# Masked attention and a rational FFN on one Trainium2 core: the rational function in monic form with three buffers per group, a constant scale in the mask, and a new order

## The chip, the cores and the metric

The kernel runs on one core of one Trainium2 chip. The metric is the device time in microseconds (us) of one execution; less is better. The engines of a core work side by side and are named as in the profile: PE is the matmul engine (PEld its weight load), DVE the vector engine, ACT the scalar engine, POOL the GpSimd engine, SP the sync engine, which here only issues DMAs.

## The reference

Two stages, on q, k, v of shape (8, 8, 576, 64): batch, heads, positions, head width. The arrays and the result are 32-bit floats.

```python
scores = scale * q @ k.T                        # per batch and head, 576 x 576, scale = 1/8
thresh = max(scores) - tau                      # per row, tau = 0.02
scores = where(scores >= thresh, scores, -1e9)
attn = exp(scores - max(scores))
attn = attn / (sum(attn) + 1e-9)
x = attn @ v                                    # 4608 tokens x 512

h = x @ w_in                                    # 512 x 2048
P = a0 + a1*h + a2*h**2 + a3*h**3
Q = 1 + |b0|*|h| + |b1|*h**2
g = P / (Q + 1e-6)
out = g @ w_out                                 # 2048 x 512
```

## The kernel before, in words

**Attention.** A unit is a pair of heads and a block of 128 query rows (`full`, both heads together), or the 64 rows that are left of 576 (both heads in one). `f_qk` (lines 734 to 757) makes the scores in three PSUM banks, `f_max` (763, 765) takes the negated row maximum, and `f_thr` (767 to 772) turns it into the number that the mask needs. `f_pre` (774 to 778) applies the mask with one Prelu of a huge slope: what lies over the threshold stays as it is, what lies below becomes hugely negative. `f_sum` (780 to 782) takes the exponential in place and sums each row on the way; its bias `ntau` shifts the kept scores back. `f_rec` and `f_rec2` make the reciprocal of the sum. Then the weights are split in two 16-bit parts, `hi` (`f_hi`, helper line 300 or 302) and `lo` (`f_lo`, 804), transposed by DMA on SP's queue (`f_tp`, 814), and multiplied by the split V (`f_av`, 873). The first batch, whose pairs are `plain`, does it with PE transposes and 32-bit matmuls instead (lines 817 to 857). `f_xh` and `f_xl` put the result into an x chunk: 256 token columns of all four head pairs.

**Weights.** w_in and w_out arrive as 64-bit words and are decoded on ACT and DVE in pieces of 128 rows (`decode_ops`, 422 to 474), sixteen of each; POOL issues their loads (490, 529). w_in is scaled and split into two 16-bit parts, every second row block of w_out into two parts of another format.

**FFN.** `moe_ops` (957 to 1154) works on a group: one x chunk and four blocks of 128 columns of w_in, so 128 x 1024 numbers of h. `f_g1` (988) makes h in PSUM, `f_h` (997) scales it into a buffer `t`. Then comes the rational function on 128 x 1024: `f_A` |h| (1002 on ACT or 1004 on DVE); `f_t1` b1 |h| + b0 (1009 or 1011); `f_r` a3 h + a2 (1016 or 1018); `f_r2` (helper line 307) and `f_r3` (1033) the rest of the numerator; `f_q` (1024) the rest of the denominator; `f_ln` and `f_inv` (1027, 1030) a first reciprocal as exp(-ln Q); `f_e`, `f_n` (1036, 1039) one Newton step on it; `f_g` (1042) the quotient, negated. `f_gh`, `f_gl` split half of it, and `f_g2` (1059, 1063) multiplies by w_out into two accumulators, one per 128 tokens, over all sixteen blocks of a chunk. `f_o` (1068, 1073) takes the sum out with a factor of -1, `f_st` stores it. A group takes four `t` buffers here (h, A, q, r), of ten, which it shares with the weight loads.

**The order.** It is worked out when the program is built. Every step is an `op` with an engine (or several with a duration on each, the table `FLEX`), a duration, a due time `key` in units of attention blocks, the steps it follows, and the buffers and PSUM banks it takes and gives back (`Hold`). `Plan.order` (148 to 243) runs a list schedule over these numbers: at each step the engine that can begin first takes, among what can begin about then (`TOL`), the step with the smallest key; a step with several engines goes to the one where `sooner` sees an earlier, priced end (`EARLY` until `EARLY_END`, then `PRICE`). Each engine then executes its steps in that order. Where PE would stand idle before `WARM_END`, dummy matmuls are put in (line 1205). `LEAD`, `SPACE0`, `SPACING`, `ENDK`, `ENDS`, `WHEN` and `AHEAD_RANK` set the due times of FFN groups and weights; `BA`, `BH` and `B1` list the PSUM banks that accumulators, h and other results may take; `plan.rank` sets who is served first with buffers.

Of the kernel before, what the change touches and what calls it, by code (L numbers as in the profile page):

```python
# [19 lines left out]
QC = 1.0 + 1e-6  # L20

POOLS = {"e": 3, "hi": 2, "pT": 2, "st": 8, "sc": 2, "t": 10, "u": 3, "g": 2, "x": 3, "xr": 1}
# [29 lines left out]
STEEP = 2.0 ** 100  # L54

PLAIN = (0, 1, 2, 3, 4)

UP = 2.0 ** -14
TPD = 1.3

AHEAD_RANK = 2.6933

# [8 lines left out]
        "ev": {"ACT": 0.465, "DVE": 0.6}, "ev1": {"ACT": 0.156, "DVE": 0.196}, "A": {"ACT": 0.583, "DVE": 0.341},  # L71
        "r": {"ACT": 0.666, "DVE": 0.4015}, "r2": {"DVE": 0.6075},
# [6 lines left out]
TOL = {"PE": 0.08, "ACT": 0.129, "DVE": 0.1, "POOL": 0.1, "DMA": 0.0, "GD": 0.0}  # L79
WARM, WARM_END = 0.6, 400.0  # L80
# [170 lines left out]
def masked_attention_rational_ffn(  # L251
# [16 lines left out]
    P = 128  # L268
# [37 lines left out]
    def tensor_tensor(dst, x, y, how):  # L306
        engines[plan.eng].tensor_tensor(dst, x, y, how)  # L307
# [10 lines left out]
    def place(h):  # L318
        return places[h.pool][h.slot]
# [9 lines left out]
    cv = cf[:, 8:16]  # L329
    qscale, taue = cv[:, 2:3], cv[:, 3:4]  # L330
    ident = const.tile([P, P], F32, name="ident")
# [3 lines left out]
    ones = bass.AP(one.tensor, one.offset, [list(one.ap[0]), [0, P]])  # L335
    qc = cv[:, 5:6]
    nc.vector.memset(qc, QC)

# [6 lines left out]
    for t in KKs:  # L345
        nc.gpsimd.memset(t[0:D, S:QW], 0.0)
        nc.gpsimd.memset(t[D:P, 0:REM], 0.0)
    nc.vector.tensor_scalar(qscale, cf[:, 6:7], 0.0, SCALE, ALU.is_ge, ALU.mult)
    nc.vector.tensor_scalar(cv[:, 4:5], cf[:, 6:7], 0.0, None, ALU.is_lt)
    nc.vector.scalar_tensor_tensor(taue, cf[:, 6:7], 0.0, cv[:, 4:5], ALU.max, ALU.add)  # L350

    nc.vector.tensor_scalar(taue, taue, 110.0, None, ALU.min)
    ntau = cv[:, 6:7]
    nc.vector.tensor_scalar(ntau, taue, -1.0, None, ALU.mult)
    a0, a1, a2, a3 = (cf[:, i:i + 1] for i in range(4))
    b0, b1 = cv[:, 0:1], cv[:, 1:2]

    def load_coefficients():
# [6 lines left out]

    def scale_ops(key, get, up, inv, s, after, tag):


        box = {}
        plan.rank = key  # L370
        h, hd, hb = Hold("sc", 1), Hold("u", 1), Hold("b", 1, B1)
# [104 lines left out]
    def w_key(i, j):  # L476
        k, step = WHEN[i]
        return k + j * step
# [3 lines left out]
    for i in range(NW):  # L482
# [18 lines left out]
        key = w_key(i, NC)  # L501
        sd = scale_ops(key, lambda i=i: wm[:, i * NC:(i + 1) * NC], 14, sw[:, i:i + 1], sw[:, NW + i:NW + i + 1], [x[3] for x in pieces], f"w{i}")
        sw_done.append(sd)
# [124 lines left out]
    def load_v_ops(bp):  # L628
# [35 lines left out]
        if pr == NP - 1:  # L664
            isx_done[bb] = scale_ops(p if bb else 4.0, lambda: vms[bb], 14, isx[:, bb:bb + 1], sx[:, bb:bb + 1], vm_ops[bb], f"x{bb}")
# [31 lines left out]
    xh_hold = {}  # L697
    x_done = {}

# [11 lines left out]
    def unit_ops(bp, t):  # L711
# [18 lines left out]
        def ev(hh):  # L730
            e = box["e"][:, hh * S:(hh + 1) * S]
            return e
# [34 lines left out]
        def f_thr(h0, h1):  # L767
            d, m = box["st"][:, 2 + h0:2 + h1], box["st"][:, h0:h1]
            if plan.eng == "ACT":
                nc.scalar.activation(d, m, AF.Identity, scale=qscale, bias=taue)  # L770
            else:
                nc.vector.tensor_scalar(d, m, qscale, taue, ALU.mult, ALU.add)  # L772

        def f_pre(hh):

            if hh == 0:
                box["e"] = place(e_hold)
            nc.scalar.activation(ev(hh), box["s"][hh], AF.Prelu, scale=qscale, bias=box["st"][:, 2 + hh:3 + hh], alpha=STEEP)  # L778
# [163 lines left out]
        if plain:  # L942
            av = op("PE", 2.36 if full else 0.76, p + 1.2, f_avp, two["tp"] + [v_loaded[bp]], [bh] + first, [two["pT"], vh_[bp]])
            plain_av.setdefault(bp, []).append(av)
        else:
            av = op("PE", 1.86 if full else 0.69, p + 1.2, f_av, two["tp"] + [v_low(bp)], [bh] + first, [two["pT"], vh_[bp]])
        xh = op(FLEX["xh" if full else "xhr"], 0, p + 1.4, f_xh, [av, isx_done["up"]] + ([x_done[ck][0]] if not first else []), (), [bh])
# [5 lines left out]
    accs = {}  # L953
    last_g1, last_g2 = [], {}
    sums = {}

    def moe_ops(ck, f0, nb, p, begins, ends, soon):
# [41 lines left out]
        def f_A():  # L999
            box["A"] = place(hA)[:, 0:FW]  # L1000
            if plan.eng == "ACT":
                nc.scalar.activation(box["A"], box["h"], AF.Abs)
            else:
                nc.vector.tensor_single_scalar(box["A"].bitcast(I32), box["h"].bitcast(I32), 0x7FFFFFFF, ALU.bitwise_and)

        def f_t1():
            box["q"] = place(hq)[:, 0:FW]
            if plan.eng == "ACT":
                nc.scalar.activation(box["q"], box["A"], AF.Identity, scale=b1, bias=b0)  # L1009
            else:  # L1010
                nc.vector.tensor_scalar(box["q"], box["A"], b1, b0, ALU.mult, ALU.add)

        def f_r():
            box["r"] = place(hr)[:, 0:FW]
            if plan.eng == "ACT":
                nc.scalar.activation(box["r"], box["h"], AF.Identity, scale=a3, bias=a2)  # L1016
            else:
                engines[plan.eng].tensor_scalar(box["r"], box["h"], a3, a2, ALU.mult, ALU.add)

        def f_r2():  # L1020
            tensor_tensor(box["r"], box["r"], box["h"], ALU.mult)

        def f_q():
            nc.vector.tensor_mul(box["q"], box["q"], box["A"])  # L1024

        def f_ln():
            nc.scalar.activation(box["A"], box["q"], AF.Ln, bias=qc)

        def f_inv():
            nc.scalar.activation(box["A"], box["A"], AF.Exp, scale=-1.0)  # L1030

# [3 lines left out]
        def f_e():  # L1035
            nc.vector.scalar_tensor_tensor(box["q"], box["q"], QC, box["A"], ALU.add, ALU.mult)  # L1036

        def f_n():
            nc.vector.scalar_tensor_tensor(box["q"], box["q"], -2.0, box["A"], ALU.add, ALU.mult)

# [24 lines left out]
        def f_o(tt, old):  # L1065
            if old:
                o = old[0]["o"]
                nc.vector.scalar_tensor_tensor(o, acc[tt], -1.0, o, ALU.mult, ALU.add)
            else:
                o = place(obox[tt]["hold"])  # L1070
                if not through:
                    o = o[:, tt * DM:(tt + 1) * DM]
                nc.scalar.activation(o, acc[tt], AF.Copy, scale=-1.0)  # L1073
            obox[tt]["o"] = o
# [173 lines left out]
```

## Time and profile before

| | |
|---|---|
| median of 3 runs | 1326.07 us (1324.98 to 1326.12) |
| span of the profiled execution | 1325.7 us |
| PE busy | 1291.3 us (97%), 9144 matmuls |
| PEld busy | 873.6 us (66%) |
| DVE busy | 1227.0 us (93%), 2043 instructions |
| ACT busy | 1178.6 us (89%), 2166 instructions |
| POOL busy | 244.2 us (18%), 468 instructions |
| mean granted PE clock | 0.992 |

A group of the profile is a line of the kernel on one engine: what it writes and reads, its shapes, how often it ran (x), its busy time in all, the mean duration of one in ns, and behind the second bar how long the engine was idle just ahead of it and what ended that. `cf` holds the per-partition constants (coefficients, tau), `st` the row statistics, `t` the buffers of the FFN, `banks` PSUM. A stretch (window) lists the busy time and the number of instructions of each engine within it, the clock that PE was granted (1.00 is full), the busy share of the DMA engines and GB/s. Busy PE time contains the dummy matmuls and matmuls at a lowered clock.

### The profile page before, as it was taken

What the parts mean: (1) busy time and instruction counts of PE and PEld (TensorE: products, weight loads), DVE (VectorE), ACT (ScalarE), POOL (GpSimd) and SP (SyncE); (2) the same over time, 40 slices, a digit from 0 to 9 for tenths busy, and PEclk for the clock granted to TensorE, in tenths of its full rate; (3) what the DMA queues carried; (4) which work ended last, traced back from release to release, by engine and by line L of the source; (5) the groups of instructions that cost most, each with busy time, mean ns of one, the idle gap of its engine ahead of it and who ended that gap; (6) DMA issues with size and microseconds to landing.
All of it is one profiled execution on the core that took longest, in us unless ns stands there. A gap on an engine that the chain in (4) does not pass through costs nothing. (4 is left out here: it accounts for less than half of the span.)

```text
span 1325.7 us, 24897 instructions
## 1 busy us (share of the span) xinstructions
PE 1291.3 (97%) x9144; PEld 873.6 (66%) x9144; DVE 1227.0 (93%) x2043; ACT 1178.6 (89%) x2166; POOL 244.2 (18%) x468
## 2 busy tenths in 40 slices
PE   8989899999999999999998999999999999999998
PEld 6657576666666666666666656666666766667775
DVE  6979899999999999999998899999999999987966
ACT  7979799999998999999998799999999999985764
POOL 2110000022212221332113231322213221100000
PEclk9989999999999999999999999999999999999999
DMA  8441544565656666666647465756657674550000
GB/s 266 136 139 50 167 90 78 123 152 112 134 102 116 131 109 119 125 140 116 115 100 136 78 133 101 143 101 142 110 119 130 110 139 104 103 102 1 16 17 16
DMA packets 340586, 146.63 MB, mean 111 GB/s; under 512 B 316208, under 2 KB 323184, under 8 KB 340464
## 3 DMA queue, kind: packets, MB, share of 16 engines
q1 hardware_dynamic: 316400, 86.49, 37.1%
q0 software_dynamic: 22784, 57.31, 15.5%
q8 instruction: 72, 1.18, 0.4%
q10 hardware_dynamic: 1280, 1.25, 0.4%
q14 instruction: 50, 0.41, 0.1%
HBM read 60.30 MB, written 9.44 MB: 53 GB/s over the span
## 5 line engine op out<-in xcount | busy, mean ns | idle before, releaser
L988 PEld LDWEIGHTS <-wi 128*128 128x128 f16 x3456 | 333.5, 98 | 71.8 <-issue 34.1
L988 PE MATMUL banks<-x,wi 128*128 128x256 f16 x3072 | 360.2, 273 | 2.7 <-ACT t L997 2.7
L1063 PE MATMUL banks<-wp,t 128*128 128x512 f32 x576 | 278.9, 600 | 3.4 <-DVE t L1042 3.3
L1059 PE MATMUL banks<-wp,g 128*128 128x512 f32 x864 | 275.8, 450 | 2.1 <-DVE g L1050 1.6
L778 ACT ACTIVATE e<-banks,st,cf 128x576 f32<-128x576 f32 x288 | 234.2, 827 | 14.6 <-DVE st L772 11.8
L782 ACT ACTIVATE e<-e,cf 128x576 f32<-128x576 f32 x288 | 221.3, 775 | 0.1
L804 DVE SCALAR_TENSOR_TENSOR e<-e,st,hi 128x576 f16<-128x576 f32 x252 | 204.5, 811 | 7.6 <-ACT hi L300 6.5
L1059 PEld LDWEIGHTS banks<-wp,g 128*128 128x128 f32 x864 | 158.2, 189 | 78.2 <-issue 38.6
L763 DVE TENSOR_REDUCE st<-banks 128x2 f32<-128x1152 f32 x128 | 172.2, 1346 | 9.4 <-PE banks L757 8.4
L300 ACT ACTIVATE hi<-e,st 128x576 f16<-128x576 f32 x199 | 151.6, 769 | 30.4 <-DVE st L793 20.9
L753 PE MATMUL banks<-KK,QQ 64*128 64x512 f32 x512 | 152.4, 641 | 2.1 <-ACT e L778 1.9
L1063 PEld LDWEIGHTS banks<-wp,t 128*128 128x128 f32 x576 | 101.2, 190 | 73.3 <-issue 59.2
L997 ACT ACTIVATE t<-banks,hsc 128x512 f32<-128x512 f32 (+1 forms) x192 | 106.2, 576 | 24.1 <-PE banks L988 23.8
L873 PEld LDWEIGHTS <-V 128*64 128x64 f16 x2520 | 103.1, 111 | 29.1 <-issue 27.6
L873 PE MATMUL banks<-pT,V 128*64 128x256 f16 (+1 forms) x2520 | 120.6, 249 | 0.5 <-DVE x L889 0.5
L757 PEld LDWEIGHTS banks<-KK,QQ 128*128 128x128 f32 x256 | 38.1, 188 | 97.0 <-issue 87.9
L598 POOL DMA_DIRECT2D QQ<-in_qT_dram x42 | 22.6, 538 | 424.9 <-PE banks L744 255.3
L1042 DVE SCALAR_TENSOR_TENSOR t<-t,cf,t 128x1024 f32<-128x1024 f32 (+1 forms) x73 | 92.4, 1266 | 0.8
L1033 DVE SCALAR_TENSOR_TENSOR t<-t,cf,t 128x1024 f32<-128x1024 f32 (+1 forms) x73 | 92.3, 1265 | 0.5
L1036 DVE SCALAR_TENSOR_TENSOR t<-t,t 128x1024 f32<-128x1024 f32 (+1 forms) x73 | 87.9, 1204 | 3.4 <-ACT t L1030 3.4
L307 DVE TENSOR_TENSOR t<-t,t 128x1024 f32<-128x1024 f32 (+1 forms) x73 | 87.9, 1204 | 1.6 <-ACT t L1016 1.2
L1024 DVE TENSOR_TENSOR t<-t,t 128x1024 f32<-128x1024 f32 (+1 forms) x73 | 87.9, 1204 | 1.0 <-ACT t L1009 0.8
(124 smaller groups left out, 1816.3 us busy)
## 6 DMA issues: line engine op xcount, KB each, us to landing
t<-in_w_in_dram POOLq DMA_DIRECT2D x16, 512.0 KB, 5.6
t<-in_w_out_dram POOLq DMA_DIRECT2D x16, 512.0 KB, 4.9
out_dram<-u POOLq DMA_DIRECT2D x26, 256.0 KB, 3.1
V<-in_v_dram POOLq DMA_DIRECT2D x24, 256.0 KB, 4.0
QQ<-in_qT_dram POOLq DMA_DIRECT2D x42, 144.0 KB, 2.8
KK<-in_kT_dram POOLq DMA_DIRECT2D x42, 144.0 KB, 3.0
QQ<-in_qT_dram POOLq DMA_DIRECT2D x42, 128.0 KB, 2.7
KK<-in_kT_dram POOLq DMA_DIRECT2D x42, 128.0 KB, 2.7
```

Of the source, the lines that this page charges most:

```text
L300: nc.scalar.activation(dst, src, AF.Identity, scale=factor)
L753: nc.tensor.matmul(d, QQ[r, t * P:(t + 1) * P], KK[r, REM:S], **one)
L763: nc.vector.tensor_reduce(box["st"][:, 0:2], box["both"], AX.X, ALU.max, negate=True)
L778: nc.scalar.activation(ev(hh), box["s"][hh], AF.Prelu, scale=qscale, bias=box["st"][:, 2 + hh:3 + hh], alpha=STEEP)
L782: nc.scalar.activation(e, e, AF.Exp, bias=ntau, accum_out=box["st"][:, 4 + hh:5 + hh])
L804: nc.vector.scalar_tensor_tensor(box["lo"][:, c], ev(hh), box["st"][:, 6 + hh:7 + hh], box["hi"][:, c], ALU.mult, ALU.subtract)
L873: nc.tensor.matmul(dst, V[:, c * P + hh * D:c * P + (hh + 1) * D], rhs, start=c == 0 and n == 0, stop=c == NT and n == 2)
L988: nc.tensor.matmul(d, wi_tile(c, f0 + j, hl), x[:, c, :], start=c == 0 and n == 0, stop=c == NC - 1 and n == 2)
L997: nc.scalar.activation(box["h3"][:, 2 * k:2 * k + 2, sl], psv[:, :, sl], AF.Identity, scale=hsc[:, b2, g:g + 1])
L1042: nc.vector.scalar_tensor_tensor(box["r"], box["r"], a0, box["q"], ALU.add, ALU.mult)
L1059: nc.tensor.matmul(acc[tt], fr(g[:, x]), fr(wo[f][y]), start=begins and j == n == 0, stop=ends and j == nb - 1 and n == 2)
L1063: nc.tensor.matmul(acc[tt], box["r"][:, o:o + P], wo[f], start=begins and j == 0, stop=ends and j == nb - 1)
```

## The change

The rational function is rewritten so that the leading coefficients are 1. A small step `monic`, once at the start, divides the coefficients: numerator a_i / a3, denominator b0 / b1 and (1 + 1e-6) / b1, with guards for tiny values, and puts -a3 / b1 into `osc`. Then h (h + a2) and |h| (|h| + bc) each come out of one DVE instruction, and `f_t1` and `f_r` are gone. `f_o` multiplies by `osc` in place of -1. The reciprocal is written over `h` (`box["i"] = box["h"]`), and |h| directly into the buffer of q: a group takes three `t` buffers. For that `f_ln` now follows `f_r3`. `f_e` reads its constant from `qc`, a per-partition operand.

In attention the scale of the mask and of the threshold is the constant 1/8 instead of the per-partition `qscale`; the exponential no longer has the bias `ntau`, and takes `passes` (1 or 0, by the sign of tau) as a per-partition scale.

The order: accumulators may take banks 3, 4 and 5, no longer 6; due-time constants, engine prices, one tolerance and the assumed duration of the mask are new; FFN groups have strictly rising ranks; the first attention result that goes into an x chunk now comes ahead of the others of that chunk; the scale steps of w_in are ranked earlier.

The core of the diff:

```diff
-B2, B3, BA, B1, BH = [(0, 1, 2), (3, 4, 5)], [(0, 1, 2)], [(3,), (4,), (5,), (6,)], [(7,), (6,), (5,)], [(5,), (6,)]
+B2, B3, BA, B1, BH = [(0, 1, 2), (3, 4, 5)], [(0, 1, 2)], [(3,), (4,), (5,)], [(7,), (6,), (5,)], [(5,), (6,)]
-LEAD, SPACE0, SPACING = 2.6322, 2.8866, 2.0262
-ENDK, ENDS = 5.3663, 11.0901
-WHEN = [(-3.6826, 2.0326), (5.7416, 0.8046), (12.6147, 0.2389), (15.0409, 0.8184)]
-V0, V1 = -1.5278, 1.1622
+LEAD, SPACE0, SPACING = 2.3618, 2.8866, 2.0262
+ENDK, ENDS = 6.3041, 10.3733
+WHEN = [(-4.5639, 2.0326), (5.966, 0.8046), (12.6147, 0.2389), (15.3809, 0.834)]
+V0, V1 = -1.2774, 1.1622
-AHEAD_RANK = 2.6933
+AHEAD_RANK = 2.4556
-EARLY = {"ACT": 1.5503, "DVE": 2.8692}
-EARLY_END = 792.5446
-PRICE = {"ACT": 0.7875, "DVE": 2.2723}
+EARLY = {"ACT": 1.7178, "DVE": 2.8692}
+EARLY_END = 1001.6266
+PRICE = {"ACT": 0.885, "DVE": 2.1934}
...
+    def monic():
+        t, u, a3 = (co_[:, i:i + 1] for i in range(6, 9))
+        nc.vector.tensor_scalar(t, b0, 2.0 ** -40, TINY, ALU.mult, ALU.max)
+        nc.vector.tensor_tensor(t, b1, t, ALU.max)
+        nc.vector.reciprocal(u, t)
+        nc.vector.tensor_tensor(bc, b0, u, ALU.mult)
+        nc.vector.tensor_scalar(qc, u, QC, None, ALU.mult)
...
+        nc.vector.scalar_tensor_tensor(osc, a3, -1.0, u, ALU.mult, ALU.mult)
+        nc.vector.reciprocal(a3, a3)
+        nc.vector.tensor_scalar(co_[:, 0:3], cf[:, 0:3], a3, None, ALU.mult)
+    co = op("DVE", 2.1, 6.0, monic, [co])
...
-            nc.scalar.activation(ev(hh), box["s"][hh], AF.Prelu, scale=qscale, bias=box["st"][:, 2 + hh:3 + hh], alpha=STEEP)
+            nc.scalar.activation(ev(hh), box["s"][hh], AF.Prelu, scale=SCALE, bias=box["st"][:, 2 + hh:3 + hh], alpha=STEEP)
...
-            nc.scalar.activation(e, e, AF.Exp, bias=ntau, accum_out=box["st"][:, 4 + hh:5 + hh])
+            nc.scalar.activation(e, e, AF.Exp, scale=passes, accum_out=box["st"][:, 4 + hh:5 + hh])
...
-            ex[hh] = op("ACT", 0.716, p + 0.2 + 0.02 * hh, lambda hh=hh: f_pre(hh),
+            ex[hh] = op("ACT", 0.63, p + 0.2 + 0.02 * hh, lambda hh=hh: f_pre(hh),
...
-        plan.rank = p = max(p, w_key(g, 2 * NC) - 1.0)
+        plan.rank = p = max(p, w_key(g, 2 * NC) - 1.0, ranks[-1] + 0.01)
...
         def f_r2():
-            tensor_tensor(box["r"], box["r"], box["h"], ALU.mult)
+            box["r"] = place(hr)[:, 0:FW]
+            nc.vector.scalar_tensor_tensor(box["r"], box["h"], a2, box["h"], ALU.add, ALU.mult)
         def f_q():
-            nc.vector.tensor_mul(box["q"], box["q"], box["A"])
+            nc.vector.scalar_tensor_tensor(box["q"], box["q"], bc, box["q"], ALU.add, ALU.mult)
         def f_ln():
-            nc.scalar.activation(box["A"], box["q"], AF.Ln, bias=qc)
+            box["i"] = box["h"]
+            nc.scalar.activation(box["i"], box["q"], AF.Ln, bias=qc)
...
-                nc.scalar.activation(o, acc[tt], AF.Copy, scale=-1.0)
+                nc.scalar.activation(o, acc[tt], AF.Identity, scale=osc)
...
-        hh, hA, hq, hr = Hold("t", 1), Hold("t", 1), Hold("t", 1), Hold("t", 2 * nb)
+        hh, hq, hr = Hold("t", 1), Hold("t", 1), Hold("t", 2 * nb)
...
-        A = op(can("A"), 0, p + 0.55, f_A, [h], [hA])
-        t1 = op(can("r"), 0, p + 0.56, f_t1, [A], [hq])
-        r = op(can("r"), 0, p + 0.6, f_r, [A], [hr])
-        r2 = op(can("r2"), 0, p + 0.6, f_r2, [r])
-        q = on("DVE", 0.6075, p + 0.65, f_q, [A, t1])
-        ln = on("ACT", 0.632, p + 0.7, f_ln, [q])
+        A = op(can("A"), 0, p + 0.55, f_A, [h], [hq])
+        r2 = on("DVE", 0.638, p + 0.6, f_r2, [h], [hr])
+        q = on("DVE", 0.638, p + 0.65, f_q, [A])
+        r3 = on("DVE", 0.638, p + 0.67, f_r3, [r2])
+        ln = on("ACT", 0.632, p + 0.7, f_ln, [q, r3])
         iv = on("ACT", 0.563, p + 0.75, f_inv, [ln])
-        r3 = on("DVE", 0.638, p + 0.8, f_r3, [r2], (), [hh])
         e = on("DVE", 0.6075, p + 0.85, f_e, [iv])
-        nn = on("DVE", 0.6075, p + 0.9, f_n, [e], (), [hA])
+        nn = on("DVE", 0.6075, p + 0.9, f_n, [e], (), [hh])
         gd = on("DVE", 0.638, p + 0.95, f_g, [nn, r3], (), [hq])
```

More of the change, by code (lines that the diff above doesn't have):

```diff
@@ L54 @@
 STEEP = 2.0 ** 100
+ALL = 2.0 ** 100
 PLAIN = (0, 1, 2, 3, 4)
@@ L71 @@
         "ev": {"ACT": 0.465, "DVE": 0.6}, "ev1": {"ACT": 0.156, "DVE": 0.196}, "A": {"ACT": 0.583, "DVE": 0.341},
-        "r": {"ACT": 0.666, "DVE": 0.4015}, "r2": {"DVE": 0.6075},
         "gh": {"ACT": 0.31, "DVE": 0.2}, "wh": {"ACT": 0.57, "DVE": 0.38}}
-EARLY = {"ACT": 1.5503, "DVE": 2.8692}
-EARLY_END = 792.5446
-PRICE = {"ACT": 0.7875, "DVE": 2.2723}
-TOL = {"PE": 0.08, "ACT": 0.129, "DVE": 0.1, "POOL": 0.1, "DMA": 0.0, "GD": 0.0}
+EARLY = {"ACT": 1.7178, "DVE": 2.8692}
+EARLY_END = 1001.6266
+PRICE = {"ACT": 0.885, "DVE": 2.1934}
+TOL = {"PE": 0.08, "ACT": 0.1241, "DVE": 0.1, "POOL": 0.1, "DMA": 0, "GD": 0}
 WARM, WARM_END = 0.6, 400.0
@@ L329, in masked_attention_rational_ffn @@
     cv = cf[:, 8:16]
-    qscale, taue = cv[:, 2:3], cv[:, 3:4]
+    passes, taue = cv[:, 2:3], cv[:, 3:4]
     ident = const.tile([P, P], F32, name="ident")
@@ L347, in masked_attention_rational_ffn @@
         nc.gpsimd.memset(t[D:P, 0:REM], 0.0)
[L348 to L355, printed above, removed]
+    nc.vector.tensor_scalar(passes, cf[:, 6:7], 0.0, None, ALU.is_ge)
+    nc.vector.tensor_scalar(cv[:, 4:5], cf[:, 6:7], 0.0, ALL, ALU.is_lt, ALU.mult)
+    nc.vector.tensor_scalar(taue, cf[:, 6:7], 0.0, 80.0, ALU.max, ALU.min)
+    nc.vector.tensor_tensor(taue, taue, cv[:, 4:5], ALU.add)
     b0, b1 = cv[:, 0:1], cv[:, 1:2]
+    co_ = const.tile([P, 12], F32, name="co")
+    a0, a1, a2 = (co_[:, i:i + 1] for i in range(3))
+    bc, qc, osc = (co_[:, i:i + 1] for i in range(3, 6))
     def load_coefficients():
@@ L501, in masked_attention_rational_ffn @@
         key = w_key(i, NC)
-        sd = scale_ops(key, lambda i=i: wm[:, i * NC:(i + 1) * NC], 14, sw[:, i:i + 1], sw[:, NW + i:NW + i + 1], [x[3] for x in pieces], f"w{i}")
+        sd = scale_ops(key, lambda i=i: wm[:, i * NC:(i + 1) * NC], 14, sw[:, i:i + 1], sw[:, NW + i:NW + i + 1], [x[3] for x in pieces], AHEAD_RANK)
         sw_done.append(sd)
@@ L769, in f_thr @@
             if plan.eng == "ACT":
-                nc.scalar.activation(d, m, AF.Identity, scale=qscale, bias=taue)
+                nc.scalar.activation(d, m, AF.Identity, scale=SCALE, bias=taue)
             else:
-                nc.vector.tensor_scalar(d, m, qscale, taue, ALU.mult, ALU.add)
+                nc.vector.tensor_scalar(d, m, SCALE, taue, ALU.mult, ALU.add)
         def f_pre(hh):
@@ L999, in f_A, with f_r2 @@
         def f_A():
[L1000 to L1006, printed above, removed]
             box["q"] = place(hq)[:, 0:FW]
             if plan.eng == "ACT":
-                nc.scalar.activation(box["q"], box["A"], AF.Identity, scale=b1, bias=b0)
+                nc.scalar.activation(box["q"], box["h"], AF.Abs)
             else:
-                nc.vector.tensor_scalar(box["q"], box["A"], b1, b0, ALU.mult, ALU.add)
-        def f_r():
+                nc.vector.tensor_single_scalar(box["q"].bitcast(I32), box["h"].bitcast(I32), 0x7FFFFFFF, ALU.bitwise_and)
+        def f_r2():
             box["r"] = place(hr)[:, 0:FW]
[L1015 to L1020, printed above, removed]
-            tensor_tensor(box["r"], box["r"], box["h"], ALU.mult)
+            nc.vector.scalar_tensor_tensor(box["r"], box["h"], a2, box["h"], ALU.add, ALU.mult)
         def f_q():
-            nc.vector.tensor_mul(box["q"], box["q"], box["A"])
+            nc.vector.scalar_tensor_tensor(box["q"], box["q"], bc, box["q"], ALU.add, ALU.mult)
         def f_ln():
-            nc.scalar.activation(box["A"], box["q"], AF.Ln, bias=qc)
+            box["i"] = box["h"]
+            nc.scalar.activation(box["i"], box["q"], AF.Ln, bias=qc)
         def f_inv():
-            nc.scalar.activation(box["A"], box["A"], AF.Exp, scale=-1.0)
+            nc.scalar.activation(box["i"], box["i"], AF.Exp, scale=-1.0)
         def f_r3():
```

31 lines of the change are left out of this document (19 added, 12 removed).

## The prediction

> **What bounds the kernel now.** I read the busy time by stage first, cut where the character of the work changes: weight decoding and the first attention units until 200 us, the mixed stretch, the disturbed stretch from 690 to 800 us, the mixed stretch again, and the last FFN groups alone from 1193 us. The columns are the stretch, its length, the busy time of each engine with its instructions, the granted clock, and the DMA share.
>
> ```profile
> 0.00:200.00 200.00, 181.39 (x1249) 130.77 (x1249) 170.76 (x388) 169.68 (x351) 26.39 (x67) 0.96 0.50 140
> 200.00:690.00 490.00, 486.16 (x3505) 322.18 (x3504) 479.31 (x767) 459.93 (x836) 104.14 (x192) 1.00 0.60 119
> 690.00:800.00 110.00, 103.87 (x755) 67.91 (x752) 100.44 (x173) 96.29 (x187) 28.37 (x52) 0.98 0.57 111
> 800.00:1193.00 393.00, 391.62 (x2884) 260.92 (x2884) 377.56 (x602) 373.23 (x673) 85.32 (x157) 1.00 0.62 118
> 1193.00:1325.70 132.70, 128.25 (x764) 91.79 (x758) 98.90 (x117) 79.44 (x123) 0.00 (x0) 1.00 0.04 13
> sum 1325.70, PE 1291.29 PEld 873.57 DVE 1226.97 ACT 1178.58 POOL 244.22; mean PE 258.26 PEld 174.71 DVE 245.39 ACT 235.72 POOL 48.84
> ```
>
> The reader sees PE idle for 1325.7 - 1291.3 = 34.4 us in all: 18.6 before 200 us, 3.8 to 690, 6.1 to 800, 1.4 to 1193, and 4.4 at the end. From 200 to 1193 us all three engines are nearly full. From 1193 us PE alone is.
>
> Busy PE time is not all useful: the plan fills PE's early waits with dummy matmuls (line 1205). Their row for the first 200 us, same columns without the other engines:
>
> ```profile
> 0.00:200.00 200.00, 27.80 (x182) 25.24 (x182) 0.96 0.50 140
> ```
>
> So before 200 us PE loses 18.6 idle, 27.8 in fillers and, at a granted clock of 0.96, about another 8: some 54 us of 200. There ACT and DVE (85% busy each) and their latencies set the pace. Everywhere later PE sets it, and what a lighter ACT and DVE can return there is only the small losses: 3.8 + 6.1 + 1.4 of idle time and 2.2 for the clock of 0.98 over 110 us, together 13.5 us.
>
> The Trainium skill (Trainium Kernel Development and Optimization, Performance Expectations) calls matmul busy time a bad measure of the distance from the limit. The rows agree: busy time leaves 18.6 us of room before 200 us, the filler and clock rows some 54. This bears on the chance of the large gain below, which the 18.6 alone would hardly allow.
>
> **The change part by part.** No matmul of the model is added or removed, so PE's own work stays. The prices on ACT:
>
> ```profile
> L778 ACT ACTIVATE e<-banks,st,cf 128x576 f32<-128x576 f32 x288 | 234.2, 827 | 14.6 <-DVE st L772 11.8 <-DMA pT<-e 1.3 <-issue 0.5
> ...
> L1027 ACT ACTIVATE t<-t,cf 128x1024 f32<-128x1024 f32 (+1 forms) x73 | 82.7, 1132 | 4.2 <-DVE t L1024 3.9
> L1030 ACT ACTIVATE t<-t 128x1024 f32<-128x1024 f32 (+1 forms) x73 | 75.8, 1039 | 0.3
> L1002 ACT ACTIVATE t<-t 128x1024 f32<-128x1024 f32 (+1 forms) x63 | 66.0, 1048 | 0.6
> L1009 ACT ACTIVATE t<-t,cf 128x1024 f32<-128x1024 f32 (+1 forms) x52 | 63.8, 1228 | 0.5
> ...
> L1016 ACT ACTIVATE t<-t,cf 128x1024 f32<-128x1024 f32 (+1 forms) x38 | 46.5, 1223 | 0.0
> L770 ACT ACTIVATE st<-st,cf 128x2 f32<-128x2 f32 (+1 forms) x105 | 39.9, 380 | 11.9 <-DVE st L763 11.7
> ...
> L1073 ACT ACTIVATE u<-banks 128x512 f32<-128x512 f32 x34 | 19.9, 590 | 6.0 <-PE banks L1059 5.8
> ```
>
> *Passes.* `f_t1` and `f_r` go: 63.8 + 46.5 = 110.3 us of ACT. *Constant scale.* The rows price a per-partition operand: Ln with one takes 1132, Exp with none 1039 (93 ns); Identity with two takes 1228, Abs with none 1048 (90 ns each). The mask (line 778) loses one of its two: 288 x 0.09 = 25.9 us. That is the same instruction at a shape that no row shows with one operand fewer, so the bounds are nothing and 288 x 0.093 = 26.8; I take 25.9 because both pairs agree. The threshold on ACT (line 770) loses one as well, 105 x 0.09 = 9.4. The Exp of line 782 swaps its bias operand for a scale operand: nothing, and if the two differ, at most the same 0.09 in either direction. The output eviction (line 1073) gains one: 34 x 0.09 = 3.1. ACT in all: 110.3 + 25.9 + 9.4 - 3.1 = 142.5 us less, from 1178.6 to about 1036.
>
> ```profile
> L1033 DVE SCALAR_TENSOR_TENSOR t<-t,cf,t 128x1024 f32<-128x1024 f32 (+1 forms) x73 | 92.3, 1265 | 0.5
> L1039 DVE SCALAR_TENSOR_TENSOR t<-t,t 128x1024 f32<-128x1024 f32 (+1 forms) x73 | 88.0, 1205 | 0.6
> L1024 DVE TENSOR_TENSOR t<-t,t 128x1024 f32<-128x1024 f32 (+1 forms) x73 | 87.9, 1204 | 1.0 <-ACT t L1009 0.8
> ...
> L1018 DVE TENSOR_SCALAR t<-t,cf 128x1024 f32<-128x1024 f32 (+1 forms) x35 | 28.0, 801 | 16.9 <-ACT t L997 16.9
> ...
> L793 DVE RECIPROCAL st<-st 128x2 f32<-128x2 f32 (+1 forms) x160 | 25.2, 157 | 5.7 <-ACT st L787 4.9
> ...
> L1011 DVE TENSOR_SCALAR t<-t,cf 128x1024 f32<-128x1024 f32 (+1 forms) x21 | 16.7, 797 | 4.6 <-ACT t L1002 4.5
> ```
>
> On DVE the share of the two passes goes, 28.0 + 16.7 = 44.7. But `f_q`, `f_r2` and `f_e` turn from forms of 1204 ns into the form with an operand of 1265: 3 x 73 x 0.06 = 13.1 more. `monic` adds fourteen tiny instructions once, at the 0.157 of the reciprocal 2.2 us. DVE: 29.4 us less, to about 1197.6. So the relief is on ACT; DVE shares it only where the plan hands flexible steps (`hi`, `thr`, `f1`, `gh`) over to ACT.
>
> *Where it counts: before 200 us.* Of the removed work this lies there (the first three rows are ACT's, the last is DVE's):
>
> ```profile
> L778 ACT ACTIVATE e<-banks,st,cf 128x576 f32<-128x576 f32 x44 | 36.6, 842 | 11.4 <-DVE st L772 11.3
> ...
> L1009 ACT ACTIVATE t<-t,cf 128x1024 f32<-128x1024 f32 x4 | 4.9, 1237 | 0.1
> ...
> L1016 ACT ACTIVATE t<-t,cf 128x1024 f32<-128x1024 f32 x2 | 2.5, 1234 | 0.0
> ```
>
> ```profile
> L1018 DVE TENSOR_SCALAR t<-t,cf 128x1024 f32<-128x1024 f32 x2 | 1.6, 806 | 0.0
> ```
>
> ACT loses 4.9 + 2.5 + 44 x 0.09 = 11.4. DVE loses 1.6 and gains 2.2 from `monic` and 0.5 from three groups: 1.1 more. Net 10.3 of 170.8 + 169.7 = 340.5 us. If both share it and dead time shrinks along, 200 x 10.3 / 340.5 = 6 us. Ends: nothing, even 1.1 us lost, if DVE sets the pace; 11.4 if ACT alone does. I take 6, because both are equally busy there.
>
> *Three buffers.* Groups and weight loads share the ten `t` buffers, and a load can stand long in POOL's queue, with the loads behind it:
>
> ```profile
> POOL t L529 <- ACT t L1027: 27.7, 1, 27.7
> ```
>
> One buffer fewer per group can bring such loads forward. What of the 27.7 us would reach PE no row shows; between 0 and the 11 us or so that the earlier terms leave of the 18.6 us idle. I take 2, near the lower end, since ACT and DVE, 85% busy, have to do the decoding all the same.
>
> *The small losses from 200 to 1193 us.* Most of these gaps follow a late ACT or DVE; with ACT at 1036 of 1326 they should shrink. Bounds 0 and 13.5; I take 8, because the largest is a transpose's (below).
>
> *Dearer.* The accumulators lose bank 6. If PE has to stand behind an eviction at each change of chunk, the 34 evictions, two to a chunk, make it 17 x 0.59 = 10.0 us; the plan knows the banks and can put other matmuls there, so between 0 and 10.0, and I take 2. `f_ln` overwrites `h` and so has to wait for `f_r3`: two DVE passes (2.5 us) enter the chain to Ln, `f_t1` (1.2) leaves it. Behind Ln on ACT stand evictions and masks, but the plan orders ACT with that dependence, and three groups fit into nine buffers, as little more than two did in ten; nothing is counted. If the cover fails, it shows at the very end alone, as some 1.3 us of latency.
>
> The sum against the profiled execution: 1325.7 - 6 - 2 - 8 + 2 = 1311.7; the median of the runs lies 0.4 above that span, so 1312.
>
> **The rivals.** *A, the forecast*, 1312, with its own range 1303 to 1319 (the early term between 2 and 9, the late one between 5 and 13).
>
> *B, DVE keeps the pace.* DVE is as busy as ACT in every stage and is hardly relieved, early not at all. Then the early term is -1, the buffers give nothing and the late losses return 4: 1323. For it: 1197.6 us of DVE work against 1036 on ACT. Against it: the plan has flexible steps in plenty.
>
> *C, the early stretch gives way.* ACT sets the pace early (11.4), the buffers give 5, the late losses 12, the banks cost nothing: 1326.1 - 28.4 = 1298. For it: the 54 us lost there.
>
> *D, pile-ups of transfers.* The order is set anew, and transposes may meet loads more often. The one in the trace (SP's transposes, and what ACT and PE waited for):
>
> ```profile
> 723.91 2.84 SPq L814 DMA_TRANSPOSE pT<-hi  x1
> ...
> 727.23 0.77 ACT L300 ACTIVATE hi<-e,st 128x576 f16<-128x576 f32 x1 [3.67 <-DMA pT<-hi]
> ...
> 728.84 2.56 PE L988 MATMUL banks<-xr,wi 128*128 128x256 f16 x13 [3.32 <-ACT t L997]
> ```
>
> A transpose of `hi` is slow, ACT stands 3.67 us for its buffer, everything queued behind it on ACT stands too, and PE waits 3.32 us for an eviction of `h`. The stretch around it lost 6.1 idle and 2.2 by the clock: 8.3 us. Faster masks bring transposes closer together. Two more such stretches (16.6) eat the gain; three give 1312 + 25 = 1337. Against it: from 800 to 1193 us the DMA share is higher (0.62 against 0.57) and PE loses only 1.4 us.
>
> The Trainium skill (Trainium Kernel Development and Optimization, Key Constraints) says that transfers issued from SP, ACT and GpSimd run on the same DMA engines and interleave. The slow transpose beside the loads agrees with that; by this rule alone a denser order would be slower, as in D.
>
> **How the numbers follow.** A measurement of this kernel tells 0.2%, 2.65 us, from no change: faster is below 1323.4, slower above 1328.7. Chances: A 0.53, B 0.19, C 0.18, D 0.10. B lies at the border of faster and the same: half of it to each. Faster 0.53 + 0.18 + 0.09 = 0.80, the same 0.10, slower 0.10. The range leaves out D and the lower half of C, 0.19: 1297 to 1326.
>
> **What would show it.** Lines of `f_t1` and `f_r` gone; the mask at about 737 ns; ACT about 140 us less busy, less what the plan moves there from DVE; PE full by about 193 us instead of 200, with fewer fillers; PE's idle time between 200 and 1193 us near 5 instead of 11.3 us. Wrong it would be if the mask stays at 827, if the first FFN groups begin no earlier than before, or if PE shows new gaps behind an eviction (banks) or behind `hi` (transposes).

## The result, and the profile after

| | before | after |
|---|---|---|
| median | 1326.09 us (1324.98 to 1328.51) | 1314.53 us (1311.82 to 1315.60) |
| ratio | 1 | 0.9904, 95% interval 0.9886 to 0.9922 |
| span of the profiled execution | 1325.7 us | 1313.8 us |

The change makes the kernel faster by 1.0%. (The two medians alone give a ratio of 0.9913, inside the interval.) Medians in this document are of all executions; ratios and intervals leave out the few in which the whole program ran far longer, such as one of 1605.71 us among the twelve of the run with both below. The profiled executions differ by 11.9 us. The busy times of after in the same stretches, then the dummy matmuls in the first two of them (columns as in the prediction):

```profile
0.00:200.00 200.00, 182.20 (x1251) 129.53 (x1252) 176.91 (x407) 161.29 (x350) 30.75 (x73) 0.97 0.49 141
200.00:690.00 490.00, 488.57 (x3519) 322.98 (x3518) 470.29 (x747) 422.39 (x820) 106.85 (x197) 1.00 0.64 121
690.00:800.00 110.00, 108.95 (x832) 73.30 (x831) 103.00 (x167) 94.54 (x195) 30.17 (x56) 1.00 0.60 120
800.00:1193.00 393.00, 390.44 (x2876) 259.39 (x2875) 365.02 (x568) 329.65 (x641) 80.18 (x149) 1.00 0.59 112
1193.00:1313.80 120.80, 115.14 (x641) 80.81 (x639) 85.38 (x96) 56.59 (x92) 0.00 (x0) 1.00 0.04 14
```

```profile
0.00:200.00 200.00, 25.72 (x166) 23.35 (x166) 0.97 0.49 141
200.00:690.00 490.00, 0.39 (x2) 0.30 (x2) 1.00 0.64 121
```

What PE loses is a stretch's length less its busy time, plus the fillers, plus the part of a slower clock. Before and after, in us:

| stretch | idle | fillers | clock | lost before | lost after |
|---|---|---|---|---|---|
| to 200 | 18.6, 17.8 | 27.8, 25.7 | 8, 6 | 54.4 | 49.5 |
| 200 to 690 | 3.8, 1.4 | 2.5, 0.4 | 0, 0 | 6.3 | 1.8 |
| 690 to 800 | 6.1, 1.0 | 0, 0 | 2.2, 0 | 8.3 | 1.0 |
| 800 to 1193 | 1.4, 2.6 | 0, 0 | 0, 0 | 1.4 | 2.6 |
| the end | 4.4, 5.7 | 0, 0 | 0, 0 | 4.4 | 5.7 |

The gain, 14.2 us by this rough account and 11.9 by the spans, has three parts: 4.9 before 200 us, 4.5 in the first long mixed stretch, and 7.3 where before had its disturbed stretch. 2.5 us are lost again later. (The clock is given to two places, so its column is good to a microsecond or so. Over the executions of before the mean clock varies from 0.987 to 0.997, so the 4.2 us of the gain that stand in this column are the least certain.)

The groups of after that answer to the priced steps, ACT's first (line 801 is the mask, 1040 the Ln, 793 the threshold, 1086 the eviction), then DVE's (1049 is `f_e`, 1033 `f_r2`, 1036 `f_q`):

```profile
L801 ACT ACTIVATE e<-banks,st 128x576 f32<-128x576 f32 x288 | 206.2, 738 | 17.4 <-DVE st L795 12.0 <-DMA pT<-e 2.1 <-issue 0.8
...
L1040 ACT ACTIVATE t<-t,co 128x1024 f32<-128x1024 f32 (+1 forms) x73 | 82.6, 1132 | 36.3 <-DVE t L1046 36.2
...
L793 ACT ACTIVATE st<-st,cf 128x2 f32<-128x2 f32 (+1 forms) x105 | 30.4, 289 | 36.6 <-DVE st L786 34.3 <-DVE st L788 2.1
...
L1086 ACT ACTIVATE u<-banks,co 128x512 f32<-128x512 f32 x34 | 23.0, 683 | 7.8 <-PE banks L1072 7.8
```

```profile
L1049 DVE SCALAR_TENSOR_TENSOR t<-t,co,t 128x1024 f32<-128x1024 f32 (+1 forms) x73 | 92.2, 1263 | 30.5 <-ACT t L1043 30.5
L1046 DVE SCALAR_TENSOR_TENSOR t<-t,co,t 128x1024 f32<-128x1024 f32 (+1 forms) x73 | 92.1, 1262 | 0.0
L1033 DVE SCALAR_TENSOR_TENSOR t<-t,co 128x1024 f32<-128x1024 f32 (+1 forms) x73 | 92.1, 1262 | 2.2 <-ACT t L1022 2.2
L1036 DVE SCALAR_TENSOR_TENSOR t<-t,co 128x1024 f32<-128x1024 f32 (+1 forms) x73 | 92.1, 1261 | 0.0
```

The mask takes 738 ns (737 was forecast), the threshold 289 instead of 380, the eviction 683 instead of 590. Behind the second bar stands what the freed load became: idle time. The Ln, which was hardly waited for (4.2 us), now sits idle 36.3 us for `f_r3` (line 1046), and `f_e` 30.5 us for the exponential. Little of it reaches PE: PE waits for `f_g`, the last step of the chain, 2.1 us in all (before: 3.3), and 1.0 of that lies at the very end. The longest of these waits:

```profile
1302.63 1.55 PE L1076 MATMUL banks<-wp,t 128*128 128x512 f32 x3 [0.65 <-DVE t L1055]
```

### The profile page after: what moved, and what is told of

Its sections match the earlier page's. It is cut to its first block, busy times and chain, and to the rows that moved or that the text cites. A ratio compares the mean times of both kernels' runs of the same rounds, so it can differ in the third digit from the quotient of the medians.

```text
span 1313.8 us, 24744 instructions
## 1 busy us (share of the span) xinstructions
PE 1285.3 (98%) x9112; PEld 866.0 (66%) x9112; DVE 1200.6 (91%) x1981; ACT 1064.5 (81%) x2094; POOL 248.0 (19%) x474
## 5 line engine op out<-in xcount | busy, mean ns | idle before, releaser
L1013 PEld LDWEIGHTS <-wi 128*128 128x128 f16 x3456 | 332.7, 98 | 64.8 <-issue 27.7
L801 ACT ACTIVATE e<-banks,st 128x576 f32<-128x576 f32 x288 | 206.2, 738 | 17.4 <-DVE st L795 12.0
L303 ACT ACTIVATE hi<-e,st 128x576 f16<-128x576 f32 x192 | 144.7, 769 | 52.0 <-DVE st L816 42.3
L896 PEld LDWEIGHTS <-V 128*64 128x64 f16 x2520 | 102.9, 111 | 28.9 <-issue 25.7
L1049 DVE SCALAR_TENSOR_TENSOR t<-t,co,t 128x1024 f32<-128x1024 f32 (+1 forms) x73 | 92.2, 1263 | 30.5 <-ACT t L1043 30.5
L1040 ACT ACTIVATE t<-t,co 128x1024 f32<-128x1024 f32 (+1 forms) x73 | 82.6, 1132 | 36.3 <-DVE t L1046 36.2
L1033 DVE SCALAR_TENSOR_TENSOR t<-t,co 128x1024 f32<-128x1024 f32 (+1 forms) x73 | 92.1, 1262 | 2.2 <-ACT t L1022 2.2
L1055 DVE SCALAR_TENSOR_TENSOR t<-t,co,t 128x1024 f32<-128x1024 f32 (+1 forms) x73 | 92.2, 1264 | 0.8
L1046 DVE SCALAR_TENSOR_TENSOR t<-t,co,t 128x1024 f32<-128x1024 f32 (+1 forms) x73 | 92.1, 1262 | 0.0
```

Source lines behind the costliest of these rows:

```text
L303: nc.scalar.activation(dst, src, AF.Identity, scale=factor)
L801: nc.scalar.activation(ev(hh), box["s"][hh], AF.Prelu, scale=SCALE, bias=box["st"][:, 2 + hh:3 + hh], alpha=STEEP)
L896: nc.tensor.matmul(dst, V[:, c * P + hh * D:c * P + (hh + 1) * D], rhs, start=c == 0 and n == 0, stop=c == NT and n == 2)
L1013: nc.tensor.matmul(d, wi_tile(c, f0 + j, hl), x[:, c, :], start=c == 0 and n == 0, stop=c == NC - 1 and n == 2)
L1049: nc.vector.scalar_tensor_tensor(box["q"], box["q"], qc, box["i"], ALU.add, ALU.mult)
```

## The experiments

Two theories go through the experiments. L: the lighter ACT and DVE give the gain. O: the new order gives it. In all of them the ratio is to the kernel before, run beside them.

### The old order with the new work

Each step keeps the place that the plan of before gave it. In place of the two removed passes nothing is issued:

```diff
 def f_t1():
     box["q"] = place(hq)[:, 0:FW]
-    nc.scalar.activation(box["q"], box["A"], AF.Identity, scale=b1, bias=b0)
 def f_r2():
-    tensor_tensor(box["r"], box["r"], box["h"], ALU.mult)
+    nc.vector.scalar_tensor_tensor(box["r"], box["h"], a2, box["h"], ALU.add, ALU.mult)
 def f_q():
-    nc.vector.tensor_mul(box["q"], box["q"], box["A"])
+    nc.vector.scalar_tensor_tensor(box["q"], box["A"], bc, box["A"], ALU.add, ALU.mult)
```

`f_r` is treated as `f_t1`, and where these two ran on DVE, DVE's form is left out in the same way; `f_o` and `f_e` take `osc` and `qc` as in after; the coefficients are divided right behind the step that takes the absolute value of b. Monic form alone:

> The order of before, kept as it is, with the monic form put into it: the steps f_t1 and f_r keep their places and issue nothing, f_r2 and f_q are the new single instructions, the coefficients are divided once; the mask keeps its per-partition scale, four buffers per group stay. Theory L (the lighter ACT and DVE give the gain): most of the 110 us of ACT and 30 us of DVE is off PE's path, but the small losses shrink, about 1319 us. Theory O (the new order gives the gain): the old order keeps its places of loss, 1324 to 1327 us.

Measured: 1329.92 us, 1.0026 (1.0015 to 1.0037). Constant scale alone, which changes line 778, the threshold, the exponential and the few steps that set up their constants:

> The order of before, kept as it is, with the constant scale in mask and threshold and the exponential without shift; the rational function as before. The mask should take about 737 ns instead of 827, ACT 35 us less in all. Theory L: a quarter of what the whole load relief gives, 1323 us. Theory O: 1325 to 1327 us.

Measured: 1323.17 us, 0.9969 (0.9957 to 0.9981); the mask took 733 ns. Both:

> The order of before with both: monic form and constant scale, so the work of after in the old order, with four buffers per group. Theory L: about the time of after, 1314 to 1317 us, and the gap of 3.3 us of PE near 728 us gone or halved. Theory O: 1322 to 1326 us, with that gap as before.

Measured: 1326.07 us, 0.9998 (0.9985 to 1.0011). The time is in the range of O, but the gap is not as before: it is about halved, as L had it. (`hi` on ACT, then PE's matmul behind the gap.)

```profile
729.74 0.77 ACT L302 ACTIVATE hi<-e,st 128x576 f16<-128x576 f32 x1 [2.22 <-DMA pT<-hi]
731.26 1.91 PE L1012 MATMUL banks<-xr,wi 128*128 128x256 f16 x16 [1.78 <-ACT t L1021]
```

PE stands 1.78 us there (at 731 us in this run) instead of 3.32, and is idle 4.6 us from 690 to 800 us instead of 6.1; but it is idle 6.4 us from 200 to 690, instead of 3.8. To see whether the place of the division spoils it, it was moved to the first `f_t1`:

> The same as the run with both in the old order, but the fourteen instructions that divide the coefficients come just ahead of the first use of them on DVE, near 105 us, instead of at the very start, where DVE stood for the coefficients' DMA and everything behind them was late. Theory L (load gives gain in the old order too): the 4 to 5 us that the earlier run lost in its first 50 us come back, so about 1320 us. Theory O (only a new order turns the freed load into time): 1324 to 1327 us.

Measured: 1323.62 us, 0.9983 (0.9972 to 0.9995). The reason given there does not hold: in the earlier two runs the fourteen instructions ran on DVE from 41 to 44 us without a gap. What parts the two kernels, 2.4 us, is less than the 0.2% that a measurement here can tell, and its cause stays open.

With all of the new work in the old order, ACT's busy time falls to 1058.9 us (after: 1064.5), and most of PE's losses stay. The late stretches of the last run:

```profile
200.00:690.00 490.00, 485.44 (x3502) 322.18 (x3501) 467.73 (x741) 415.83 (x804) 104.01 (x192) 1.00 0.61 119
690.00:800.00 110.00, 105.18 (x763) 68.77 (x761) 99.50 (x170) 86.82 (x181) 28.80 (x53) 0.98 0.59 112
```

PE is idle 4.6 us until 690 us (before: 3.8) and 4.8 until 800 (6.1), though ACT has 44 us less to do in the first of them. From 200 to 1193 us PE is idle 9.9 us in this run and 11.5 in the one before it; before it was 11.3. So all of the lighter work, taken alone, explains 0 to 2 us of the 12. By the ratios, constant scale alone gave 4 and the monic form alone lost 3; why the second takes the gain of the first away is not shown.

### The new order with the old work

```diff
 def f_A():
+    nc.scalar.activation(box["q"], box["h"], AF.Identity, scale=osc, bias=bc)
     nc.scalar.activation(box["q"], box["h"], AF.Abs)
 def f_r2():
     box["r"] = place(hr)[:, 0:FW]
+    again[0] += 1
+    if again[0] % 2:
+        nc.scalar.activation(box["r"], box["h"], AF.Identity, scale=osc, bias=a2)
+    else:
+        nc.vector.tensor_scalar(box["r"], box["h"], osc, a2, ALU.mult, ALU.add)
```

Where the step of |h| runs on DVE, the added pass is DVE's form; the per-partition scale is back in mask and threshold.

> The order of after, kept as it is, with the old load put back: the mask and threshold with a per-partition scale, and two more passes per group (one with the step of |h| on its engine, one ahead of f_r2, alternately on ACT and DVE), whose results are overwritten. So about the work of before in the new order with three buffers. Theory L: the gain goes, 1324 to 1332 us, since the new order was made for shorter steps. Theory O: most of the gain stays, 1315 to 1319 us.

Measured: 1458.14 us, 1.0986 (1.0970 to 1.1003), far beyond both. The edit is not only load. Every second pass ahead of `f_r2` is on ACT, while `f_r2` is on DVE: a wait between engines that the plan knows nothing of. It is the longest wait of DVE in this kernel (line 1043 is `f_r2`, 1040 the added ACT pass):

```profile
DVE t L1043 <- ACT t L1040: 85.3, 35, 5.4
```

So this run cannot price the load: an unplanned wait is mixed into it. The clean part of it, the scale of mask and threshold alone, adds no wait:

> The order of after, kept as it is, with only the per-partition scale put back into mask and threshold: 26 + 9 us of ACT, no new wait between engines. Theory L: a part of the gain goes that is in proportion to the load, some 2 to 4 us, so 1317 to 1319 us. Theory O with a fragile order (each step that runs longer than the plan holds delays what is queued behind it): 1320 us or more. If ACT's slack takes it all: 1314 to 1316 us.

Measured: 1319.44 us, 0.9950 (0.9935 to 0.9965): 4.9 us more than after (6.1 by the ratios), between the ranges of the two theories. ACT still had slack, its busy time was 1096.3 of 1318 us, and yet 0.09 us more per mask, where the plan counts on 0.63, cost about half of the gain. PE is idle 33.5 us instead of 28.5, a little more in every stretch but the last. So within this order the lighter work does count: an order that was planned for short steps is paid for when a step is longer.

### The constants and the code apart

The due times, prices, the tolerance and the accumulators' banks were exchanged between the two kernels, and the order planned anew in each. The code of after holds, besides the lighter work and the third buffer, its new rules of order (rising ranks, the first attention result of a chunk ahead, earlier scale steps), so "code" here is not the load alone.

```diff
-LEAD, SPACE0, SPACING = 2.3618, 2.8866, 2.0262
-ENDK, ENDS = 6.3041, 10.3733
+LEAD, SPACE0, SPACING = 2.6322, 2.8866, 2.0262
+ENDK, ENDS = 5.3663, 11.0901
...
```

> The code of after with the due times, prices, tolerance and accumulator banks of before; the order is planned anew with them. Theory L: the plan uses the lower load by itself, 1315 to 1319 us. Theory O (the retuned constants give it): 1322 us or more.

> The code of before with the due times, prices, tolerance and accumulator banks of after; planned anew. Theory L: no gain without the lighter steps, 1325 to 1332 us. Theory O: 1316 to 1321 us.

| | constants of before | constants of after |
|---|---|---|
| code of before | 1 | 1329.72 us, 1.0025 (1.0009 to 1.0040) |
| code of after | 1328.15 us, 1.0010 (0.9996 to 1.0024) | 1314.53 us, 0.9904 (0.9886 to 0.9922) |

Neither half gains anything; together they gain 1%. Theory L and theory O both fall in the form in which they were put: the new code with the old constants came out in the range of O, the old code with the new constants in that of L. The code of after with the old constants, by stretches:

```profile
0.00:200.00 200.00, 183.09 (x1268) 132.13 (x1270) 175.49 (x402) 164.25 (x355) 28.38 (x72) 0.97 0.51 141
200.00:690.00 490.00, 485.26 (x3508) 320.41 (x3507) 468.39 (x734) 417.90 (x818) 105.93 (x195) 1.00 0.62 121
690.00:800.00 110.00, 107.05 (x784) 70.73 (x783) 97.45 (x160) 89.70 (x187) 31.74 (x58) 0.97 0.63 116
800.00:1193.00 393.00, 386.97 (x2856) 256.75 (x2856) 362.34 (x555) 338.63 (x660) 80.28 (x149) 1.00 0.59 114
```

Its first 200 us are no worse than those of after (16.9 us idle at a clock of 0.97). It loses the time late: 4.7 us idle until 690, 2.9 idle and 3.3 by the clock until 800, 6.0 idle behind that, against 1.4, 1.0 and 2.6 in after.

The code of before with the new constants does the same. Its first stretches, then its dummy matmuls in the first:

```profile
0.00:200.00 200.00, 184.39 (x1292) 132.25 (x1293) 176.45 (x395) 172.61 (x358) 24.29 (x63) 0.97 0.48 141
200.00:690.00 490.00, 482.06 (x3461) 318.06 (x3460) 475.49 (x773) 454.40 (x811) 106.00 (x192) 1.00 0.61 119
690.00:800.00 110.00, 104.28 (x802) 69.33 (x801) 102.64 (x171) 100.61 (x204) 33.42 (x60) 1.00 0.60 125
```

```profile
0.00:200.00 200.00, 28.04 (x196) 26.31 (x196) 0.97 0.48 141
```

What PE loses in the first 200 us, by the account of the result, and the time at which the first Ln of an FFN group begins, in us:

| kernel | idle | fillers | clock | lost | first Ln |
|---|---|---|---|---|---|
| before | 18.6 | 27.8 | 8 | 54.4 | 111.3 |
| old order, new work | 19.3 | 28.1 | 10 | 57.4 | 115.2 |
| the same, division late | 19.6 | 28.4 | 6 | 54.0 | 112.8 |
| code of before, constants of after | 15.6 | 28.0 | 6 | 49.6 | 101.8 |
| code of after, constants of before | 16.9 | 26.1 | 6 | 49.0 | 106.8 |
| after | 17.8 | 25.7 | 6 | 49.5 | 102.5 |

The old, heavier work has the whole early gain once it is planned anew, and the lighter work in the old order has none of it. So in the first 200 us, too, it is the order that gives the gain, and lighter steps are neither needed for it nor enough.

### One constant nudged

```diff
-LEAD, SPACE0, SPACING = 2.3618, 2.8866, 2.0262
+LEAD, SPACE0, SPACING = 2.4018, 2.8866, 2.0262
```

> The code of after with one due-time constant nudged, LEAD 2.3618 to 2.4018, so another order of the same work. If the gain belongs to the lighter work: 1312 to 1318 us. If much of it belongs to the one order that the constants pick: 1318 us or more, as scattered as the order with the old constants (1328). Either way the gain in the first 200 us should stay (about 3 us by the work that PE has done).

Measured: 1349.53 us, 1.0178 (1.0154 to 1.0203). The same work with due times of the FFN groups 0.04 units later is slower than the kernel before by 1.8%. The late stretches:

```profile
200.00:690.00 490.00, 480.39 (x3455) 317.35 (x3454) 463.36 (x726) 408.42 (x794) 105.45 (x192) 1.00 0.62 119
690.00:800.00 110.00, 106.62 (x806) 71.92 (x806) 96.23 (x161) 89.65 (x186) 28.38 (x52) 0.97 0.61 110
800.00:1193.00 393.00, 385.22 (x2778) 253.42 (x2776) 365.32 (x570) 332.32 (x647) 82.68 (x155) 0.99 0.61 114
1193.00:1347.80 154.80, 145.46 (x867) 103.72 (x864) 103.49 (x121) 73.85 (x123) 1.12 (x2) 0.99 0.09 21
```

PE idles 9.6, 3.4, 7.8 and 9.3 us in them, where after idles 1.4, 1.0, 2.6 and 5.7: 19.4 us more. Some 9 us more go by the lower clock of the last three. The first 200 us are as in after (182.14 us busy). What PE waits for is spread over `f_g`, the masks and the evictions of h:

```profile
PE banks L1076 <- DVE t L1055: 8.2, 9, 3.5
PE banks L776 <- ACT e L801: 7.9, 6, 2.6
PE banks L1013 <- ACT t L1022: 6.0, 7, 2.1
```

So late in the kernel it is the single order that decides, by more than the whole gain.

### Bank 6, and a fourth buffer

```diff
-B2, B3, BA, B1, BH = [(0, 1, 2), (3, 4, 5)], [(0, 1, 2)], [(3,), (4,), (5,)], [(7,), (6,), (5,)], [(5,), (6,)]
+B2, B3, BA, B1, BH = [(0, 1, 2), (3, 4, 5)], [(0, 1, 2)], [(3,), (4,), (5,), (6,)], [(7,), (6,), (5,)], [(5,), (6,)]
```

> The code of after with bank 6 given back to the accumulators, planned anew. If the missing bank costs PE waits behind evictions, as the 2 us of the prediction have it: 1312 to 1314 us. If it costs nothing, only another order: anywhere between 1314 and 1328, as scattered as the other orders, with no wait of PE for an eviction in either.

Measured: 1314.06 us, 0.9897 (0.9880 to 0.9914). Each engine's instructions stand in exactly the same order as in after: with bank 6 the plan comes out the same. The missing bank costs nothing here, and the run repeats after, 0.5 us apart.

```diff
-hh, hq, hr = Hold("t", 1), Hold("t", 1), Hold("t", 2 * nb)
+hh, hA, hq, hr = Hold("t", 1), Hold("t", 1), Hold("t", 1), Hold("t", 2 * nb)
...
-    box["i"] = box["h"]
+    box["i"] = place(hA)[:, 0:FW]
...
-ln = on("ACT", 0.632, p + 0.7, f_ln, [q, r3])
+ln = on("ACT", 0.632, p + 0.7, f_ln, [q], [hA])
...
-nn = on("DVE", 0.6075, p + 0.9, f_n, [e], (), [hh])
+nn = on("DVE", 0.6075, p + 0.9, f_n, [e], (), [hA])
```

> The code of after with a fourth buffer per group: the reciprocal gets its own, taken by the Ln, which no longer waits for f_r3; planned anew. If the third buffer is worth the 2 us of the prediction or more: weight loads stand longer and the first 200 us lose 2 us or more against after. If it is worth nothing there: the first FFN groups begin within 2 us of after, and the time differs only by the scatter of orders, 1314 to 1328.

Measured: 1341.83 us, 1.0108 (1.0090 to 1.0126). Not early, though:

```profile
0.00:200.00 200.00, 182.23 (x1295) 130.76 (x1296) 182.07 (x414) 166.78 (x360) 29.66 (x72) 0.99 0.51 143
...
690.00:800.00 110.00, 97.50 (x711) 64.59 (x710) 92.19 (x152) 80.19 (x164) 28.32 (x52) 0.95 0.64 107
```

With four buffers the first 200 us lose less by the clock than in after (0.99 against 0.97) and no more in idle time; the first Ln begins at 96.7 us instead of 102.5, and the longest stand of a weight load in POOL's queue is 14.5 us instead of 17.4. The loss is late again, 12.5 us idle from 690 to 800. Whether the fourth buffer or just the other order does that, one run cannot tell.

### The pile-up of transfers

```diff
 def ld():
     t = Vs[vhold.slot]
+    if bp == 21:
+        nc.gpsimd.memset(t, 0.0)
+        return
     queue.dma_start(
```

> The order of before, kept as it is; the V load near 720 us (the second pair of the sixth batch) is left out, POOL sets that V to zero instead, so 288 KB fewer move while three transposes are under way. That V's part of the result is not computed. Theory T (the loads make the transposes late, and these make PE wait): the 3.3 us gap of PE near 728 us goes or shrinks to under 1 us, the time falls by 3 to 8 us, to 1318 to 1323. Theory Q (ACT's and DVE's queues are late by themselves there): gap and time as before.

Measured: 1324.85 us, 0.9987 (0.9973 to 1.0000). The time alone is hardly told from no change: 1.7 us by the ratio, not the 3 to 8 of theory T. The trace shows the mechanism. SP's transposes, the step of `hi` on ACT, and PE, in this run:

```profile
723.68 1.32 SPq L817 DMA_TRANSPOSE pT<-hi  x1
...
724.39 0.78 ACT L300 ACTIVATE hi<-e,st 128x576 f16<-128x576 f32 x1 [0.26 <-DMA pT<-hi]
```

```profile
722.65 6.98 PE L991 MATMUL banks<-xr,wi 128*128 128x256 f16 x60
```

The transpose takes 1.32 us instead of 2.84, ACT waits 0.26 instead of 3.67, and PE runs through sixty matmuls where it had stood for 3.32 us. From 690 to 800 us PE is busy 107.65 us at the full clock, instead of 103.87 at 0.98. So the loads beside the transposes made that gap, by one profiled execution of each kernel; the time of the whole program did not follow it in full.

After has such a meeting too. V loads and transposes fall together at 722 us, and one transpose takes 2.60 us:

```profile
723.59 2.60 SPq L837 DMA_TRANSPOSE pT<-e  x1
...
727.42 1.96 PE L1072 MATMUL banks<-wp,g 128*128 128x512 f32 x6
...
727.58 0.78 ACT L303 ACTIVATE hi<-e,st 128x576 f16<-128x576 f32 x1 [2.25 <-DMA pT<-hi]
...
729.23 2.79 PE L1013 MATMUL banks<-x,wi 128*128 128x256 f16 x24
```

ACT stands 2.25 us for the same buffer, and PE goes from one matmul to the next, since the groups of w_out that stand in its queue there had their inputs ready. The pile-up is not gone; it is covered.

## Why the prediction was right, and where its reasons were not

The time, 1312 against 1314.5, and the direction were right, and the range held. The prices of the steps were right. The two terms that make up the gain, 6 early and 8 late, have the right size for a reason that the runs do not bear out: both were put down to lighter steps, and both came with the new order. That the sum fits is in this part luck. The terms:

- **The prices.** Right to a few ns: mask 738, threshold 289, eviction 683, the DVE forms 1261 to 1263. By groups ACT loses 110.3 + 288 x 0.089 + 105 x 0.091 - 34 x 0.093 = 142.3 us, as forecast. Its busy time falls by less, 1178.6 to 1064.5 (about 1036 forecast): the durations of all its instructions add up to 139 us less, but busy time counts the overlap of two neighbours once, and that overlap shrank from 199 to 174 us. DVE falls from 1227.0 to 1200.6 (1197.6 forecast).
- **Before 200 us.** 6 forecast, 4.9 by the account above. The size fits, the reason does not. Every order that was planned anew has this gain, the one with the old work too (49.6 us lost there, after 49.5); the new work in the old order does not have it (54.0 and 57.4, before 54.4). The prediction took ACT's and DVE's load for what sets the pace there; at that load a new order was enough. Which of the new due times gives it is open.
- **Three buffers, 2.** Not borne out. The longest stand of a weight load in POOL's queue went from 27.7 to 17.4 us, but the kernel with four buffers had 14.5 and no worse a start.
- **The late losses, 8.** 4.5 + 7.3 - 1.2 = 10.6 us by the account, of which 2.1 are fewer dummy matmuls, which the prediction left out; in its own terms, idle time and clock, 13.5 became 5.0, so 8.5 less. The size fits, the reason does not. The prediction said that these gaps "should shrink" because ACT is lighter. In the old order the same lighter work halved the gap near 728 us and left the idle time of the whole late part at 9.9 to 11.5 us (before 11.3), and with the old constants or with one constant nudged they came back larger. This is the step that failed, here as before 200 us: it took a loss of one particular order for a loss of load.
- **The banks, 2.** Nothing: with or without bank 6 the order is the same, and PE waits for no eviction of an accumulator in after.
- **The chain to Ln, nothing counted.** The cover did fail at the very end, as the prediction allowed: 5.7 us idle there against 4.4, and 1.0 of it in two gaps behind `f_g`, near the 1.3 named. Elsewhere it is mostly idle time of ACT.
- **Rival D**, on the other side, was given 0.10. Its mechanism is real, and slow orders are close: four of the newly planned ones came out between 1328 and 1350 us. But pile-ups are not shown to be what slows them: PE's and ACT's waits for transposes add up to 3 to 7 us in each of the four, which lose 14 to 35 against after; in after they are 4.3 us, all on ACT. That after did not come out slow is a property of its constants, which nothing in the profile of before could show.
- **The signs.** PE's idle time from 200 to 1193 us came to 5.0 us, where near 5 was forecast, and the fillers are fewer. That the first FFN groups begin earlier is true of their Ln (102.5 us against 111.3) and not of the first matmul that makes h (85.3 against 80.4).
- **Two sums.** By their terms A's own range begins at 1304, not 1303, and the 1323 of B leaves out the 2 us of the banks. Neither changes the forecast.

What stays open: why an order nudged by so little loses 35 us, beyond the list of its waits, and how many sets of constants would do as well as these; no run tried more of them. A version faster than after did not come out of the runs (bank 6 gives the same program).

## What to carry to other kernels

With an order that is planned ahead, lighter steps and a new order have to be measured apart: keep the order and change the work, keep the work and change the order, and nudge one constant to see how far orders scatter (here by more than the gain). Where PE is nearly full, work taken from other engines gave next to no time by itself here, not even in the first 200 us, where those engines are 85% busy; it gave time in an order that was made for it. A stretch that looks bound by load can be bound by its order: the same load, planned anew, tells. In an experiment that puts work back, look first for a wait between engines that the edit adds.

## What the runs showed of the hardware

- A per-partition operand costs an ACT instruction 89 to 93 ns at each of three shapes: 827 to 738 at 128 x 576, 380 to 289 at 128 x 2, 590 to 683 at 128 x 512 (there Copy became Identity as well).
- Transposes on SP's queue slow down beside loads: issue of 2.84 us beside V, Q and K loads, 1.32 us at the same place without the V load (one execution each).
